# Chunk 1's second product by seven products of quarters, four more blocks transposed by DMA, and new instruction orders, in a decayed-attention and feed-forward kernel

## The chip, the cores and the metric

One Trainium2 chip, one core of it. The metric is device time in microseconds. The kernel before took 211.13 us (median of 3 runs, 210.77 to 211.39).

## The reference

Two stages. The first is causal linear attention with decay for 4 batches, 8 heads, 768 positions, head size 64, in blocks with a running state; the second is a feed-forward layer on the result, seen as 3072 tokens of 512 values.

```python
for b in range(nb):
    intra = np.einsum('bhic,bhjc->bhij', qb, kb) * Dmask[None]
    intra = np.einsum('bhij,bhjd->bhid', intra, vb)
    inter = np.einsum('bhid,bhde->bhie', qb * lam_pow[None], kv_state)
    out[:, :, sl] = intra + inter
    kv_state = lam_block * kv_state + np.einsum('bhsd,bhse->bhde', kb * rev_pow, vb)
x = out.transpose(0, 2, 1, 3).reshape(B * S, H * D)
h = x @ w_in                       # 3072 x 512 by 512 x 2048
s = np.sin(alpha * h)
g = h + s * s / (alpha + 1e-09)
return g @ w_out                   # 3072 x 2048 by 2048 x 512
```

## The kernel before

The tokens are cut into 24 blocks of 128 (6 to a batch) for the attention and into 6 chunks of 512 (4 blocks each) for the feed-forward layer.

**A block of attention.** SP loads q, k and v in float32. `scale_block` (L454 to 496) multiplies q and k by powers of the decay into bfloat16 (`qk2`) and casts v (`v2`). q and k are then transposed into `qkT`: on TensorE, by `piece_Q` (a pair of blocks, L519) and `piece_T` (k of one block, L498) with an eviction each, or, for blocks from `TD` on, by one `dma_start_transpose` on SP (L501). On TensorE follow S (k by q, `part_S`, L612), the masking of S on VectorE (L623, tile `Sm`), the state update Z (L656) with a copy of the state (`Zd`, `Zc`), and the output O (from the state, L694 or L707, and from `Sm`, L716), which is evicted into `xT`, the chunk's input to the feed-forward layer. The first four blocks, one chunk, go through a form of their own (`piece_K`, `piece_P`, `piece_I`) in which tokens are interleaved.

**A unit of the first product.** `unit_A` (L807) multiplies 128 columns of w_in by the 512 tokens of a chunk (4 matmuls, L822); `unit_A2` (L845) does two times 128 columns for 256 tokens (8 matmuls, L856). The result lies in a PSUM bank; ScalarE takes the sine (tile `t16`, L832 and L866), ScalarE or GpSimd squares it (`u16`, L836, L837, L870, L871), and VectorE adds it up into `gT` (L839, L874), after which the bank is free. A chunk has 16 units.

**The second product.** Chunks below `SC` use `unit_B` (L880): for 128 tokens four pieces of 4 matmuls, 512 wide (L887), a copy into `osb` (L901) and a store. Chunks from `SC` on use a product of 2 x 2 quarters with seven products (`unit_P`, L955): 14 pieces of 8 matmuls, 256 wide (L975). It needs sums of quarters of w_out (`weight_sums`, L914, operations at L930, into `ws`, `Ta` and in place in `w2`) and, for each chunk, sums of quarters of `gT` (`token_sums`, L933, operations at L953, into `Xs` and in place in `gT`; 20 for a chunk, 4 of them late). The results are put together by `finish` (L1003) through `kept`: copies (L1012), an addition (L1015) and subtractions into `osb` (L1021).

**The order.** `_Plan` records every operation with its reads and writes. The order on each of the five queues is written out as a table of operation numbers, `ORDER` (L36 to 103); a pair in TensorE's table stands for so many matmuls on an idle tile, which only keep it busy. Where an operation may go to several engines, the table decides. `_settle` merges the tables, and `emit` puts a semaphore wait before whatever reads or overwrites another queue's result. Each queue runs strictly in its order. The durations given to `op` are a planner's; they don't reach the chip.

Loads go by SP (q, k, v and the first quarter of w_in) and GpSimd's queue (the other weights, cast by DMA). Rings hold 6 blocks of k and v, 3 pairs of q, 6 scaled blocks and 6 transposed ones. The input q of the first four blocks and the first quarter of w_in, cast by `cast_w1_first` (L381), are needed before the first unit.

Of the kernel before, what the change touches and what calls it, by code (L numbers as in the profile page):

```python
# [13 lines left out]
class _Op:  # L14


    def __init__(self, eng, emit, dur, reads, writes, dma, after, issue, lat, runs=64):
# [13 lines left out]
        self.knows = None  # L31


class _Plan:
# [17 lines left out]
        ),  # L52
        "ACT": (
# [16 lines left out]
        ),  # L70
        "DVE": (
# [30 lines left out]
        ),  # L102
    }

# [104 lines left out]
def bass_lightning_attn__then__act_snake_kernel(  # L209
# [15 lines left out]
    NB = S // BL  # L225
# [1020 lines left out]
```

## Time and profile before

| | |
|---|---|
| median of the runs | 211.13 us |
| span of the profiled execution | 209.8 us |
| what the median has beyond the span | 1.3 us |
| TensorE busy | 203.5 us |
| VectorE busy | 160.3 us |
| ScalarE busy | 158.7 us |
| GpSimd busy | 126.9 us |

The page of the profile lists busy time by engine (PE is TensorE, PEld its weight loads, DVE VectorE, ACT ScalarE, POOL GpSimd, SP the queue that issues most DMAs). A group's row has line, engine, operation, output<-inputs, sizes and count, then busy us and mean ns of one, then the engine's idle time just before them with what ended it. The chain of waits gives start, length and what. A row of busy time by stretch gives the stretch, its length, then for PE, PEld, DVE, ACT and POOL the busy us (instructions), then the granted clock, the DMA engines' share and GB/s. A row in order of time gives start, length, engine, line, operation and count, with the idle time before it in brackets.

### The profile page before, as it was taken

To read this page: it belongs to the slowest core of one execution; us is meant where nothing else is said; L and a number is where in the kernel's file an instruction comes from. 1 tells how busy PE (TensorE), PEld (TensorE's weight loads), DVE (VectorE), ACT (ScalarE), POOL (GpSimd) and SP (SyncE) were. 2 spreads that over 40 slices of the span, in tenths; PEclk is the share of its full clock that TensorE was granted. 3 is DMA by queue.
4 is the path that set the end of the run, shared out by engine and by line. 5 is a ranking of instruction groups with operands and counts; after the bars stand their busy time and mean duration, and the time that the engine had idled before them with its cause. 6 is when DMAs were issued, how large, how long until landed. Compare 5 with 4: busy or idle time off the path is not lost.

```text
span 209.8 us, 4867 instructions
## 1 busy us (share of the span) xinstructions
PE 203.5 (97%) x1975; PEld 134.3 (64%) x1975; DVE 160.3 (76%) x266; ACT 158.7 (76%) x294; POOL 126.9 (60%) x130
## 2 busy tenths in 40 slices
PE   7979999999999999999998999999999999999995
PEld 6847444457677776555555667766667765666894
DVE  4884557563999866868899799889698699777643
ACT  4949995968998989999997887787963889568210
POOL 7075354994469578679885392944581957378300
DMA  4999999999998999999999920190000004000514
GB/s 141 310 318 232 206 213 237 246 229 256 220 264 205 227 245 230 223 233 196 246 271 228 213 53 0 33 271 2 3 0 3 0 23 179 3 0 0 200 40 163
DMA packets 78998, 33.35 MB, mean 159 GB/s; under 512 B 55408, under 2 KB 76160, under 8 KB 78976
## 3 DMA queue, kind: packets, MB, share of 16 engines
q1 hardware_dynamic: 73744, 27.14, 56.2%
q0 software_dynamic: 3696, 3.67, 10.5%
q10 hardware_dynamic: 1536, 2.24, 3.3%
q8 instruction: 15, 0.25, 0.5%
q14 instruction: 7, 0.06, 0.1%
HBM read 27.28 MB, written 6.29 MB: 160 GB/s over the span
## 4 chain that ended last, share of the span: by engine, by line
PE 83%; DVE 6%; DMA 3%; SPq 3%; ACT 2%; issue 1%
PE bank L822 27%; PE bank L975 22%; PE bank L887 13%; PE bank L856 10%; DMA v<-in_v_dram 3%; PE bank L716 3%; SPq L315 3%; PE bank L612 3%; DVE gT L839 2%; PE bank L694 1%; DVE Sm L623 1%; PE bank L511 1%; PE bank L656 1%; DVE w L930 1%; PE bank L534 1%; PE bank L707 1%
## 5 line engine op out<-in xcount | busy, mean ns | idle before, releaser
L822 PE MATMUL bank<-xT,w 128*128 128x512 bf16 x296 | 70.5, 379 | 0.0
L839 DVE SCALAR_TENSOR_TENSOR gT<-u,rinv,bank 128x512 bf16<-128x512 bf16 x74 | 53.6, 742 | 18.2 <-ACT u L836 12.5
L832 ACT ACTIVATE t<-bank,alpha 128x512 bf16<-128x512 f32 x74 | 50.0, 684 | 21.0 <-PE bank L822 20.5
L822 PEld LDWEIGHTS bank<-xT,w 128*128 128x128 bf16 x296 | 28.3, 98 | 28.4 <-DVE gT L839 0.4
L836 ACT ACTIVATE u<-t 128x512 bf16<-128x512 bf16 x59 | 36.5, 628 | 1.3
L837 POOL TENSOR_TENSOR u<-t 128x512 bf16<-128x512 bf16 x15 | 16.0, 1066 | 34.1 <-ACT t L832 30.5
L953 POOL TENSOR_TENSOR gT<-gT 128x512 bf16<-128x512 bf16 x24 | 27.8, 1172 | 11.2 <-DVE Xs L953 6.0
L623 DVE TENSOR_TENSOR Sm<-bank,mask 128x1024 bf16<-128x1024 f32 x24 | 29.1, 1218 | 4.3 <-PE bank L648 1.8
L887 PE MATMUL bank<-w,gT 128*128 128x512 bf16 x128 | 31.4, 380 | 0.0
L874 DVE SCALAR_TENSOR_TENSOR gT<-u,rinv,bank 128x256 bf16<-128x256 bf16 x44 | 18.8, 476 | 7.8 <-ACT u L870 6.1
L472 POOL TENSOR_TENSOR qk<-q,Lq 128x512 bf16<-128x512 f32 x20 | 21.2, 1075 | 2.8 <-DMA q<-in_q_dram 2.8
L856 PE MATMUL bank<-xT,w 128*128 128x256 bf16 x176 | 22.2, 273 | 0.0
L492 POOL TENSOR_TENSOR qk<-k,Lk 128x512 bf16<-128x512 f32 x20 | 20.9, 1053 | 0.6 <-DMA k<-in_k_dram 0.6
L866 ACT ACTIVATE t<-bank,alpha 128x256 bf16<-128x256 f32 x44 | 18.9, 476 | 2.0 <-PE bank L856 1.5
L887 PEld LDWEIGHTS bank<-w,gT 128*128 128x128 bf16 x128 | 11.7, 98 | 12.2
L856 PEld LDWEIGHTS bank<-xT,w 128*128 128x128 bf16 x176 | 16.4, 98 | 3.5 <-issue 0.3
L953 POOL TENSOR_TENSOR Xs<-gT 128x512 bf16<-128x512 bf16 x13 | 16.1, 1235 | 1.5 <-DVE gT L839 1.4
L975 PE MATMUL bank<-w,gT 128*128 128x256 bf16 (+1 forms) x136 | 16.3, 266 | 0.0
L975 PE MATMUL bank<-w,Xs 128*128 128x256 bf16 (+1 forms) x136 | 16.0, 267 | 0.1
L975 PE MATMUL bank<-ws,gT 128*128 128x256 bf16 x128 | 15.8, 273 | 0.0
L975 PEld LDWEIGHTS bank<-w,gT 128*128 128x128 bf16 x136 | 12.6, 98 | 3.2
L975 PEld LDWEIGHTS bank<-w,Xs 128*128 128x128 bf16 x136 | 12.4, 98 | 2.8 <-DVE osb L1021 0.3
(101 smaller groups left out, 276.0 us busy)
## 6 DMA issues: line engine op xcount, KB each, us to landing
q<-in_q_dram SPq DMA_DIRECT2D x12, 512.0 KB, 6.2
k<-in_k_dram SPq DMA_DIRECT2D x24, 256.0 KB, 5.5
v<-in_v_dram SPq DMA_DIRECT2D x24, 256.0 KB, 5.4
out_dram<-osb SPq DMA_DIRECT2D x14, 256.0 KB, 2.5
w<-in_moe_w_out_dram POOLq DMA_DIRECT2D x4, 512.0 KB, 11.4
w<-in_moe_w_in_dram POOLq DMA_DIRECT2D x3, 512.0 KB, 9.0
ws<-in_moe_w_in_dram SPq DMA_DIRECT2D x2, 512.0 KB, 7.5
out_dram<-osb ACTq DMA_DIRECT2D x8, 128.0 KB, 4.0
```

The source lines that it names most:

```text
L472: lambda e, a=a: e.tensor_tensor(qk2[:, j:j + 2, 4 * a:4 * a + 4, :], q32[:, jq, 4 * a:4 * a + 4, :, :].rearrange("p h t d -> p t h d"), b ...
L492: lambda e: e.tensor_tensor(qk2[:, j, H:2 * H, :], block32(k32, jl), lk, ALU.mult), 1.05,
L623: op("DVE", lambda e: e.tensor_tensor(Sm[js][:, :, :], banks[:, 512 * b0:512 * b0 + 1024].rearrange("p (c i) -> p c i", i=128), bass.AP(ma ...
L822: ins = e.matmul(ps[hb][:, c0:c1], w1[:, kc, 128 * m:128 * (m + 1)], xT[x][:, kc, c0:c1], start=(kc == 0 and c0 == lo), stop=(kc == NKC - ...
L832: op("ACT", lambda e: e.activation(t16[ju][:, w], ps[hb][:, w], ACTF.Sin, scale=alpha[:, m:m + 1]), 0.69 if hi - lo == TCH else 0.475, [ba ...
L836: lambda e: (e.activation(u16[ju][:, w], t16[ju][:, w], ACTF.Square) if e is nc.scalar else e.tensor_tensor(u16[ju][:, w], t16[ju][:, w], ...
L839: op("DVE", lambda e: e.scalar_tensor_tensor(out=gT[g][:, m, w], in0=u16[ju][:, w], scalar=rinv[:, m:m + 1], in1=ps[hb][:, w], op0=ALU.mul ...
L856: ins = e.matmul(ps[hb][:, 256 * i:256 * i + 256], w1[:, kc, 128 * (m + i):128 * (m + i + 1)], xT[x][:, kc, lo:lo + 256], start=(kc == 0 a ...
L866: op("ACT", lambda e, i=i: e.activation(t16[ju][:, 256 * i:256 * i + 256], ps[hb][:, 256 * i:256 * i + 256], ACTF.Sin, scale=alpha[:, m + ...
L887: ins = e.matmul(ps[ob][:, w], gT[g][:, m, 128 * s4:128 * (s4 + 1)], w2[:, m, w], start=(m == 0), stop=(m == NM - 1),)
L953: e.tensor_tensor(dst, in0, in1, alu), 0, rd, wr))
L975: ins = e.matmul(ps[ob][:, lo + d0:lo + d1], lhs, rhs[:, d0:d1], start=first and p == 0, stop=(p == NM // 2 - 1), skip_group_check=True)
```

## The change

Line numbers in this text are those of the kernel before; the changed file is 9 lines longer from L136 to L233 on, and 11 or more behind.

- `SC` from 2 to 1: chunk 1's second product is made by `product` in 14 pieces, with its own 20 token sums and `finish`; both sets of weight sums are made while chunk 1's first product runs, instead of in chunks 2 and 3.
- `TD` from 12 to 8: blocks 8 to 11 are transposed by DMA; a new constant `LB` keeps 12 where the loop over late blocks begins.
- Many operations may now go to other engines: q and k scalings to VectorE or GpSimd (`DP`), v casts to three engines (`ADP`), evictions and copies to ScalarE or VectorE (`AD`).
- All five tables of `ORDER` are new. In them TensorE begins with 31 idle matmuls of 512 columns where it had 42 of 112 and others between; SP loads the first k and v tiles in another sequence and issues the four new transposes between loads; GpSimd makes the decay's exponents after most of its masks; six of the ten weight sums are on GpSimd; VectorE has 295 operations where it had 266, ScalarE 290 where it had 309, GpSimd 135 where it had 132, each with issued DMAs.
- The masks' operations on half the partitions wait for GpSimd's operation before them explicitly (`some`, `strict`) instead of through a common key.

The core of the diff, without the tables:

```diff
-    TD = 12
+    TD = 8
+    LB = 12
...
-    SC = 2
-    QD = ((0, 0), (0, 2), (1, 0), (1, 2))
+    SC = 1
+    AD = (("ACT", 0, 0), ("DVE", 0, 0))
+    DP = (("DVE", 0, 0), ("POOL", 0, 0))
+    ADP = (("ACT", 0, 0), ("DVE", 0, 0), ("POOL", 0, 0))
...
-                    op("DVE",
+                    op(AD,
                        lambda e, lo=lo: (e.copy if e is nc.scalar else e.tensor_copy)(
                            w1[:, :, lo:lo + 256], ws[:, :, lo:lo + 256]), 0.7, [("ws", lo)], [("w1", lo // 256)])
...
-                op("ACT", lambda e: e.copy(osb[jo][:, w], ps[ob][:, w]), 0.59, [bank(ob)], parts)
+                op(AD, lambda e: (e.copy if e is nc.scalar else e.tensor_copy)(osb[jo][:, w], ps[ob][:, w]), 0.59, [bank(ob)], parts)
...
             pieces = pieces_of(8, None, False) + pieces_of(10, 9, False)
+            if SC == 1:
+                weight_sums(True)
+                weight_sums(False)
             for i in range(8):
                 unit_A2(1, 2 * i, 1, (5, 6, 4)[(i + 2) % 3])
+                if SC == 1 and i % 2:
+                    token_sums(1, i // 2)
...
-            block = TD
+            block = LB
             for c in range(2, NCH):
                 n, done = len(bq[c - 1]), 0
                 if c == SC:
-                    P.lead = -100
                     weight_sums(True)
-                    P.lead = 0
-                if c == SC + 1:
+                if c == SC + 1 and SC > 1:
                     weight_sums(False)
...
+        for o in order:
+            if o.eng == "POOL" and o.dma is None:
+                if last is not None and (o.some or last.some):
+                    o.strict = last
+                    o.deps.add(last)
+                last = o
```

More of the change, by code (lines that the diff above doesn't have):

```diff
@@ L31, in __init__ @@
         self.knows = None
+        self.some = False
+        self.strict = None
 class _Plan:
@@ L163, in _ordered @@
     def _ordered(d, o):
-        if d.eng != o.eng or d.dma is not None:
+        if d.eng != o.eng or d.dma is not None or d is o.strict:
             return False
@@ L446, in _ @@
             op("ACT", lambda e: e.copy(alpha[:, :], ps[4][:, 0:NM]), 0.2, [bank(4), "warm"], ["alpha"])
-            def QE(s, a):
-                return "DVE" if (s, a) in QD else "POOL"
             def ported(o):
@@ L478, in scale_block @@
                     for a in range(2) if s % 2 == 0 else ():
-                        eng, dur = ("DVE", 0.68) if s + a < 3 else ("POOL", 1.05)
-                        ported(op(eng, lambda e, a=a: e.tensor_tensor(
+                        ported(op(DP, lambda e, a=a: e.tensor_tensor(
                             qk2[:, j:j + 2, H + 4 * a:H + 4 * a + 4, :],
@@ L483, in scale_block @@
                             bass.AP(Lp, n * H + 4 * a, [[NP * H, 128], [H, 2], [1, 4], [0, D]]), ALU.mult),
-                           dur, [("k32", jl + a), "Lp"], [("k2", j, a), ("k2", j + 1, a)]))
+                           0.68, [("k32", jl + a), "Lp"], [("k2", j, a), ("k2", j + 1, a)]))
                     for a in range(2) if s % 2 == 0 else ():
-                        ported(op("ACT" if s and not a else "POOL", lambda e, a=a: (e.copy if e is nc.scalar else e.tensor_copy)(
+                        ported(op(ADP, lambda e, a=a: (e.copy if e is nc.scalar else e.tensor_copy)(
                             v2[:, j:j + 2, 4 * a:4 * a + 4, :],
@@ L490, in scale_block @@
                     return
-                ported(op("POOL",
+                ported(op(DP,
                    lambda e: e.tensor_tensor(qk2[:, j, H:2 * H, :], block32(k32, jl), lk, ALU.mult), 1.05,
                    [("k32", jl), "Lk"], [("k2", j, 0), ("k2", j, 1)]))
-                ported(op((("ACT", 0.62, 0.0), ("POOL", 1.05, 0.3)) if s > 11 else "ACT",
+                ported(op(ADP,
                    lambda e: (e.copy if e is nc.scalar else e.tensor_copy)(v2[:, j, :, :], block32(v32, jl)), 0.62,
@@ L538, in piece_Q @@
                     if len(tbs) == 2:
-                        op("ACT", lambda e, a=a: e.copy(qkT[:, jt:jt + 2, 2 * a:2 * a + 2, :], tps[a]),
+                        op(AD, lambda e, a=a: (e.copy if e is nc.scalar else e.tensor_copy)(
+                            qkT[:, jt:jt + 2, 2 * a:2 * a + 2, :], tps[a]),
                            0.59, [bank(tbs[a])], [("qT", jt, a), ("qT", jt + 1, a)])
@@ L569, in piece_K @@
                 for t in range(2):
-                    op("ACT" if s else (("DVE", 0.43, 0.0), ("ACT", 0.6, 0.0)),
+                    op(AD,
                        lambda e, t=t: (e.copy if e is nc.scalar else e.tensor_copy)(qkT[:, jt + t, 4:8, :], tps[t]),
@@ L665, in then @@
                         r = slice(64 * h, 64 * h + 64)
-                        op("ACT" if s < NP else (("ACT", 0.36, 0.0), ("DVE", 0.43, 0.0)), lambda e, r=r: (e.copy if e is nc.scalar else e.tensor_copy)(
+                        op(AD, lambda e, r=r: (e.copy if e is nc.scalar else e.tensor_copy)(
                             Zd[s % 2][r, :, r], ps[ZB][r, :].rearrange("p (a b) -> p a b", b=128)[:, :, r] if s < NB else
@@ L1011, in finish @@
                 if i in (1, 3):
-                    op("ACT", lambda e: e.copy(c1 if i == 1 else ny, got), 0.59 if n == 2 else 0.37, [bank(ob)], kc if i == 1 else kn)
+                    op(AD, lambda e: (e.copy if e is nc.scalar else e.tensor_copy)(c1 if i == 1 else ny, got), 0.59, [bank(ob)], kc if i == 1 else kn)
                     return
@@ L1199, in _ @@
                             prep(block + 2)
-                        piece_G(block if block < NBLK else None, block - 1 if block > TD else None,
+                        piece_G(block if block < NBLK else None, block - 1 if block > LB else None,
                                 3 - 3 * (done // 4 % 2) if c <= SC else other())
```

30 lines of the change are left out of this document (16 added, 14 removed), and 111 rows, old and new, of the table ORDER.

## The prediction

> **What bounds the kernel now.** I read the page first, then the chain of work in order of time, then busy time by stretch, then groups by shape.
>
> ```profile
> span 209.8 us, 4867 instructions
> PE 203.5 (97%) x1975; PEld 134.3 (64%) x1975; DVE 160.3 (76%) x266; ACT 158.7 (76%) x294; POOL 126.9 (60%) x130
> PE 83%; DVE 6%; DMA 3%; SPq 3%; ACT 2%; issue 1%
> ```
>
> ```profile
> 14.49 0.62 ACT v L486
> ...
> 19.16 0.87 PE bank L856 x8
> ...
> 39.85 0.45 PE bank L534 x8
> ...
> 52.56 0.22 PE bank L511 x4
> ...
> 81.09 1.73 PE bank L887 x8
> ...
> 136.79 0.87 PE bank L975 x8
> ...
> 193.05 14.14 PE bank L975 x152
> 207.21 0.29 DVE osb L997
> ```
>
> ```profile
> 60.00:70.00 10.00, 10.00 (x118) 7.41 (x117) 9.19 (x18) 9.13 (x20) 8.17 (x9) 1.00 0.92 225
> ...
> 100.00:110.00 10.00, 10.00 (x75) 5.29 (x73) 9.47 (x12) 9.45 (x18) 8.72 (x8) 1.00 1.20 266
> 110.00:120.00 10.00, 9.44 (x84) 6.00 (x82) 8.19 (x13) 8.18 (x14) 4.43 (x5) 1.00 1.09 227
> 120.00:130.00 10.00, 9.89 (x98) 6.43 (x97) 10.00 (x16) 7.53 (x14) 6.95 (x7) 1.00 0.19 35
> ```
>
> Three parts. Up to 19.16 us the first four blocks are loaded and attended, and TensorE waits for others (the chain runs over the last v load and ScalarE). From 19.16 to 207.21 the chain is nearly all TensorE: in the ten-microsecond stretches it idles only in 110 to 130, 0.56 + 0.11 = 0.67 us. The rest, 209.8 - 207.2 = 2.6 us, is the last subtraction and store. The clock is 1.00 throughout. The profiled execution's span of 209.8 stands 1.3 us under the median of 211.13; I take 1.3 as what lies around the span, and sum changes against the median.
>
> So there are two ways to gain: less work on TensorE, or an earlier 19.16. There is one main way to lose: another engine falls behind TensorE in the middle. That is close already: VectorE is busy 9.47 and 10.00 of 10 us in two of the stretches.
>
> **TensorE's saving.** Chunk 1's second product was 16 pieces of four 512-wide matmuls (L887); it becomes 14 pieces of eight 256-wide ones (L975). A pair of the first takes 1.73, so 16 x 0.865 = 13.84; 14 x 0.87 = 12.18. Saving 1.66 us. Blocks 8 to 11 lose two groups of eight transposes (L534, 0.45) and four of four (L511, 0.22 where nothing else delays it; one in three rows of the chain shows 0.3): 2 x 0.45 + 4 x 0.25 = 1.9 us. Together 3.56 us, all of it in the part where the chain is TensorE. It is hidden by nothing, so it counts in full as long as TensorE stays fed.
>
> **The start.** Here the new orders move work onto VectorE.
>
> ```profile
> 1.52 3.55 PE L1134 MATMUL bank<-Xs 128*128 128x112 bf16 x42 [1.52 <-DVE Xs L410]
> ...
> 5.84 2.50 DVE L462 TENSOR_TENSOR qk<-q,Lq 128x512 bf16<-128x512 f32 x4 [1.01 <-ACT Lq L434]
> ...
> 10.70 1.04 POOL L480 TENSOR_TENSOR qk<-k,Lp 128x512 bf16<-128x512 f32 x1 [5.41 <-DMA k<-in_k_dram]
> ...
> 11.27 3.49 DVE L623 TENSOR_TENSOR Sm<-bank,mask 128x1024 bf16<-128x1024 f32 x3 [0.41 <-PE bank L612]
> ...
> 13.61 0.62 POOL L486 CAST v<-v 128x512 bf16<-128x512 f32 x1 [1.31 <-DMA v<-in_v_dram]
> ...
> 15.30 1.23 DVE L623 TENSOR_TENSOR Sm<-bank,mask 128x1024 bf16<-128x1024 f32 x1 [0.54 <-PE bank L612]
> 16.89 0.79 DVE L384 CAST w<-ws 128x1024 bf16<-128x1024 f32 x1 [0.36 <-DMA ws<-in_moe_w_in_dram]
> ...
> 18.99 2.07 PE L856 MATMUL bank<-xT,w 128*128 128x256 bf16 x16
> ```
>
> Before, VectorE masks the four S tiles (L623) from 11.27 to 16.53, and GpSimd scales the last k and casts three v. After, VectorE does all four q and all four k scalings, a v cast and three evictions ahead of the first mask, then the four masks, an x eviction and the first weight cast, and only then the first unit can start. Two things set that mask. (a) VectorE's own sum: eight scalings at 2.50 / 4 = 0.63 are 5.0, the v cast, three evictions and three small casts about 2.1 (estimate from the rows of 0.42 and 0.28 of such copies): 5.84 + 7.1 = 12.9, and some 0.5 later if the exponents come later, since GpSimd now makes them after its masks. (b) The third k tile, sixth in SP's queue before (lam counted), is the ninth now. The ninth of before, a v, released GpSimd at 13.61; so the tile's scaling can start at 13.6, the other k scaling and a mask cast follow, and the first mask starts at 15.1. From there four masks (3.49 / 3 = 1.16 each, 4.65), the eviction (0.7) and the cast (0.7) take 6.05: the first unit starts at 18.95 by (a), 19.4 with the later exponents, and 21.2 by (b), against 18.99. Cost 0 to 2.2 us; I take 1.4, nearer to (b), which rests on a landing that the trace shows. The row of the 42 warming matmuls says that 512-wide ones in their place (31 of them) may hold TensorE to about 10 us, which no later step of (b) notices.
>
> **The middle.** I compare 40 units of the first product, from chunk 1's first to chunk 3's ninth, in the trace 49.55 to 121.27, counting what stands between these marks in each engine's order.
>
> ```profile
> 34.52:120.00 85.48, 84.92 (x832) 52.68 (x831) 66.71 (x109) 74.38 (x145) 61.84 (x56) 1.00 1.09 235
> 49.55:121.27 71.72, 71.16 (x724) 45.77 (x722) 58.75 (x99) 65.14 (x128) 50.24 (x47) 1.00 1.08 229
> ```
>
> ```profile
> L953 DVE TENSOR_TENSOR Xs<-gT 128x512 bf16<-128x512 bf16 x19 | 12.3, 658 | 0.1
> L726 DVE CAST xT<-bank 128x512 bf16<-128x512 f32 x7 | 5.1, 734 | 1.3 <-PE bank L716 1.1 <-PE bank L656 0.3
> L1021 DVE TENSOR_TENSOR osb<-bank,kept 128x512 f32<-128x512 f32 x6 | 4.1, 684 | 0.5 <-PE bank L975 0.5
> L666 DVE CAST Zd<-bank 64x256 bf16<-64x256 f32 x8 | 3.4, 419 | 0.2
> L930 DVE TENSOR_TENSOR w<-w 128x1024 bf16<-128x1024 bf16 x3 | 3.3, 1105 | 0.0
> L462 DVE TENSOR_TENSOR qk<-q,Lq 128x512 bf16<-128x512 f32 x4 | 2.5, 688 | 1.0 <-ACT Lq L434 1.0
> L516 DVE COPY qkT<-bank 128x512 bf16<-128x512 bf16 x5 | 2.1, 424 | 2.3 <-PE bank L511 2.3
> L543 DVE COPY qkT<-bank 128x1024 bf16<-128x1024 bf16 x3 | 2.1, 692 | 0.4 <-PE bank L534 0.4
> ```
>
> ```profile
> L953 DVE TENSOR_TENSOR gT<-gT x24: 409/418/1372, 98.2 to 200.2; 128x512 bf16<-128x512 bf16 x24
> ```
>
> TensorE needs 71.7 there. After, 24 transposes go (1.3) and the two kinds of second product nearly cancel between these marks: about 70.5. VectorE, 58.75 busy, gets 18 token sums more (8 before, 26 after), four scalings of q and k, two v casts, four operations on the products' results (chunk 1's, once ScalarE copies) and three state copies; it loses five evictions of transposes, two of x, two weight sums and a mask. With the rows: 18 x 0.42 + 4 x 0.69 + 1.2 + 4 x 0.68 + 3 x 0.42 = 15.5, less 3 x 0.42 + 2 x 0.69 + 2 x 0.73 + 0.7 + 1.1 + 1.2 = 7.1: 67.2 us if no sum is held up. The sums' row says 418 ns at the median, 658 at the mean of the other form and up to 1372: at about 0.59 each, 70.3. So **VectorE goes from 82% of this stretch to 95 to 100%**. The fullest long-lived share that the stretches show is 9.47 of 10 where TensorE never idled. At that share 67.2 takes 71.0 and 70.3 takes 74.2, that is 0.5 to 3.7 us over TensorE's 70.5. I take 1.5, nearer to the uncollided end, as the token sums are what the new order places anew. The 0.67 us of idle of before lies in this stretch and the one after and is replaced by this.
>
> ScalarE falls: it loses 12 v casts, four output copies and most of the evictions, and 65.1 of 71.7 was its load. GpSimd's total hardly changes.
>
> ```profile
> 107.05 1.16 POOL L953 TENSOR_TENSOR gT<-gT 128x512 bf16<-128x512 bf16 x1
> 107.22 1.27 DVE L953 TENSOR_TENSOR Xs<-gT 128x512 bf16<-128x512 bf16 x1
> ...
> 108.17 2.30 POOL L930 TENSOR_TENSOR w<-w 128x1024 bf16<-128x1024 bf16 x1
> ...
> 109.07 1.95 DVE L930 TENSOR_TENSOR w<-w 128x1024 bf16<-128x1024 bf16 x1
> ```
>
> These four rows show why sums take 0.42 or 1.37: a sum on VectorE that begins during GpSimd's ends some 0.3 us after GpSimd's, and the weight sum at 109.07 ends at 111.02, 0.55 after GpSimd's 110.47. So of two such operations one waits for the other. As a resource: from GpSimd's first scaling to about 120 us, GpSimd is busy 61.84 and VectorE adds some 7 of such operations, 69 of 85.5. After, GpSimd's list to the same place (15 q and 12 k scalings, 15 token and 6 weight sums, 9 casts, two squares, at the durations of before) is 67, and VectorE's (27 token and 4 weight sums, some 9 scalings and casts) 19: **86 of about 85**. [...]
>
> **DMA transposes.**
>
> ```profile
> L501 SPq DMA_TRANSPOSE qkT<-qk x12: 1239/1782/2932, 72.9 to 136.3; - x12
> ...
> DMA to landing us min/median/max: 3.1/4.6/6.7
> ```
>
> Four more of these stand in SP's queue, ahead of the v loads of blocks 9 to 11 and the k loads of 12 and 13, which wait behind them for about 4 x 1.8 = 7 us of SP's time and for GpSimd's scalings. These blocks are attended after block 8, so I cost it at nothing. The cover is that q and k of block 8 are scaled a landing (6.7 at most) before TensorE reaches its S tile; if GpSimd is late, TensorE waits for the difference. The end of the kernel holds the same 14 products of the last chunk: nothing.
>
> **Sum.** -1.66 - 1.90 + 1.4 + 1.5 - 0.67 = -1.3: 211.13 to **209.8**.
>
> **Rivals.** (1) TensorE stays dense and the start isn't late: -3.56, the idle of 0.67 gone or not, start 0 to 0.5: 207.2. For it: TensorE was never idle at a VectorE share of 10.00 in 120 to 130. Against: the start's loads. [...] (3) The DMA transposes are late: GpSimd's scaling of blocks 8 to 11 stands behind six weight sums of 2.1 us; one landing of 4.6 missed by half for two pairs gives 2 us more: 212.0.
>
> **Chances.** Forecast 0.42 (208.6 to 211.2), rival 1 0.20, rival 2 0.30, rival 3 0.08. A measurement tells about 0.3%, 0.63 us, from no change: faster is below 210.5, slower above 211.8. From the forecast 0.30, 0.09, 0.03 (faster, same, slower), rival 1 0.20 faster, rival 2 0.01, 0.03, 0.26, rival 3 0.01, 0.02, 0.05: faster 0.52, same 0.14, slower 0.34. The range is 207.0 to 213.6, from rival 1 to just past rival 2.
>
> **What would show it.** 112 more of L975's matmuls, 64 fewer of L887's, 16 fewer each of L511's and L534's; the first 256-wide unit at 19.4 to 21.2; VectorE above 93% between the marks with TensorE idle there 1 to 2 us; token sums nearer to 0.42 than 0.66. [...]

## The result and the profile after

The changed kernel takes 212.72 us (median of 6 runs, 211.87 to 213.2) against 211.14 for the kernel before (6 runs): ratio 1.0075, 95% interval 1.0057 to 1.0093. It is **slower by 0.75%**, where the prediction had 0.6% faster. Medians are over all executions of a kernel; ratios go by its fast ones, which leaves out those over 1.5% above the kernel's fastest (one each of kernels 7 and 16, three of kernel 11). Line numbers from here on are those of the changed kernel, 8 to 12 higher.

The page of the changed kernel (busy us and share by engine, and the chain that ended last by engine):

```profile
span 211.0 us, 4818 instructions
PE 201.1 (95%) x1927; PEld 135.5 (64%) x1950; DVE 167.5 (79%) x295; ACT 152.7 (72%) x279; POOL 127.9 (61%) x133
PE 69%; DVE 16%; ACT 11%; issue 2%; ACTq 0%
```

TensorE was 83% of that chain and is 69%; VectorE went from 6% to 16% and ScalarE from 2% to 11%. The work did come down, and other engines took the place. (The trace has records of 279 of the 296 matmuls of L831. The chain leaves TensorE where one is missing, so the two grown shares are likely somewhat too high.) Its start, in order of time, on TensorE, VectorE and ScalarE:

```profile
1.66 9.56 PE L1143 MATMUL bank<-Xs 128*128 128x512 bf16 x31 [1.66 <-DVE Xs L421]
...
12.20 0.42 DVE L580 COPY qkT<-bank 128x512 bf16<-128x512 bf16 x1 [0.89 <-PE bank L569]
...
15.27 4.62 DVE L632 TENSOR_TENSOR Sm<-bank,mask 128x1024 bf16<-128x1024 f32 x4
...
18.80 0.62 ACT L494 CAST v<-v 128x512 bf16<-128x512 f32 x1
19.32 1.04 ACT L395 CAST w<-ws 128x1024 bf16<-128x1024 f32 x1
20.39 0.73 ACT L748 CAST xT<-bank 128x512 bf16<-128x512 f32 x1
21.14 0.76 ACT L675 CAST Zd<-bank 64x256 bf16<-64x256 f32 x2
...
21.95 0.40 PE L788 MATMUL bank<-qkT,Zd 128*128 128x128 bf16 x4 [0.64 <-ACT Zd L675]
22.18 1.04 PE L865 MATMUL bank<-xT,w 128*128 128x256 bf16 x8
```

The first unit starts at 22.18 where it was 18.99: 3.2 us late. The 31 warming matmuls end at 11.22, VectorE waits 0.89 for the first transpose behind them, the four masks follow from 15.27, and behind them ScalarE has a cast of v, a cast of the weight, an x and two states in a row. The end, in the chain of waits:

```profile
193.55 14.92 PE bank L984 x160
...
208.50 0.29 DVE osb L1006
```

The last product ends at 208.47, where it was 193.05 + 14.14 = 207.19. So from the first unit to the last product's end it takes 186.3 where it took 188.2. By the counts TensorE has 64 fewer 512-wide matmuls at 0.216, 112 more 256-wide ones at 0.109 and 32 fewer transposes at 0.056: 13.8 - 12.2 + 1.8 = 3.4 us less to do, of which 1.9 arrived. The stretch between the marks of the prediction (chunk 1's first unit and chunk 3's ninth), and VectorE's two fullest pieces (stretch, length, busy us of PE, PEld, DVE, ACT, POOL, clock):

```profile
51.40:122.86 71.46, 69.44 (x744) 49.51 (x753) 65.81 (x122) 63.15 (x124) 53.05 (x51) 1.00 1.09 215
...
100.00:110.00 10.00, 9.24 (x100) 6.10 (x102) 9.87 (x14) 7.34 (x13) 7.88 (x9) 1.00 1.12 216
110.00:120.00 10.00, 9.39 (x82) 6.00 (x82) 9.73 (x19) 8.03 (x14) 5.20 (x6) 1.00 1.28 207
```

VectorE is at 65.81 of 71.46, 92% (82% before). In 100 to 120, where it is at 98%, TensorE idles 1.4 us, of which some 0.5 is three matmuls without a record. What TensorE waited for between 36 and 125 us (line, for what, us, times, longest):

```profile
PE bank L621 <- DVE gT L848: 0.8, 1, 0.8
PE bank L831 <- DVE gT L848: 0.5, 1, 0.5
PE bank L831 <- ACT xT L735: 0.3, 1, 0.3
...
PE bank L831 <- ACT kept L1021: 0.3, 1, 0.3
...
```

The whole list has nine, 2.7 us in all. Six of them stand where one of a unit's four matmuls has no record, while all four weight loads have: five of 0.16 us, in rows left out here, are no waits at all, and of the 0.3 for ScalarE's x, at 109.2, 0.1 is left. So TensorE waits 1.7 us there: 0.8 at 44.8, and behind chunk 1's first unit 0.3 at 100.4 for ScalarE's copy `kept`, 0.1 at 109.2 and 0.5 at 113.9 for a unit sum of VectorE. The kernel before has one there:

```profile
PE bank L694 <- DVE gT L839: 0.6, 1, 0.6
```

The token sums on VectorE and the transposes by DMA, of the changed kernel:

```profile
L962 DVE TENSOR_TENSOR gT<-gT x31: 406/420/633, 81.9 to 199.1; 128x512 bf16<-128x512 bf16 x31
...
L509 SPq DMA_TRANSPOSE qkT<-qk x16: 1243/1524/3545, 60.8 to 141.4; - x16
...
DMA to landing us min/median/max: 3.1/4.1/7.0
```

The longest such sum is 0.63 where it was 1.37, and no wait of TensorE names a transpose by DMA.

### The profile page after: what moved, and what is told of

It is laid out like the page before. It is cut to its first block, busy times and chain, and to the rows that moved or that the text cites. A ratio compares the mean times of both kernels' runs of the same rounds, so it can differ in the third digit from the quotient of the medians.

```text
span 211.0 us, 4818 instructions
## 1 busy us (share of the span) xinstructions
PE 201.1 (95%) x1927; PEld 135.5 (64%) x1950; DVE 167.5 (79%) x295; ACT 152.7 (72%) x279; POOL 127.9 (61%) x133
## 3 DMA queue, kind: packets, MB, share of 16 engines
q0 software_dynamic: 3696, 3.67, 10.8%
## 4 chain that ended last, share of the span: by engine, by line
PE 69%; DVE 16%; ACT 11%; issue 2%; ACTq 0%
PE bank L831 25%; PE bank L984 22%; PE bank L896 5%; PE bank L865 5%; PE bank L1143 5%; DVE gT L883 4%; ACT u L845 3%; DVE Sm L632 3%; ACT t L841 3%; DVE gT L848 3%; PE bank L621 2%; PE bank L725 2%; ACT Zd L675 1%; DVE Xs L962 1%; PE bank L657 1%
## 5 line engine op out<-in xcount | busy, mean ns | idle before, releaser
L831 PE MATMUL bank<-xT,w 128*128 128x512 bf16 x279 | 67.6, 379 | 2.8 <-issue 0.6
L831 PEld LDWEIGHTS bank<-xT,w 128*128 128x128 bf16 x296 | 27.6, 98 | 29.3 <-DVE gT L848 2.2
L962 POOL TENSOR_TENSOR gT<-gT 128x512 bf16<-128x512 bf16 x29 | 33.4, 1159 | 15.9 <-DVE Xs L962 7.6
L846 POOL TENSOR_TENSOR u<-t 128x512 bf16<-128x512 bf16 x12 | 12.4, 1039 | 26.2 <-ACT t L841 25.3
L984 PE MATMUL bank<-w,gT 128*128 128x256 bf16 (+1 forms) x168 | 19.9, 267 | 0.0
L984 PE MATMUL bank<-ws,gT 128*128 128x256 bf16 x160 | 19.9, 273 | 0.0
L984 PEld LDWEIGHTS bank<-w,gT 128*128 128x128 bf16 x168 | 15.9, 98 | 4.3
L500 POOL TENSOR_TENSOR qk<-k,Lk 128x512 bf16<-128x512 f32 x16 | 17.1, 1074 | 1.3 <-DMA k<-in_k_dram 1.3
L984 PEld LDWEIGHTS bank<-w,Xs 128*128 128x128 bf16 x168 | 15.8, 98 | 3.2
L984 PEld LDWEIGHTS bank<-ws,gT 128*128 128x128 bf16 x160 | 15.5, 98 | 3.5
L481 POOL TENSOR_TENSOR qk<-q,Lq 128x512 bf16<-128x512 f32 x15 | 15.5, 1042 | 0.0
L896 PE MATMUL bank<-w,gT 128*128 128x512 bf16 x58 | 14.7, 379 | 0.3
## 6 DMA issues: line engine op xcount, KB each, us to landing
w<-in_moe_w_out_dram POOLq DMA_DIRECT2D x4, 512.0 KB, 10.8
```

What stands on the lines that cost most here:

```text
L500: lambda e: e.tensor_tensor(qk2[:, j, H:2 * H, :], block32(k32, jl), lk, ALU.mult), 1.05,
L831: ins = e.matmul(ps[hb][:, c0:c1], w1[:, kc, 128 * m:128 * (m + 1)], xT[x][:, kc, c0:c1], start=(kc == 0 and c0 == lo), stop=(kc == NKC - ...
L896: ins = e.matmul(ps[ob][:, w], gT[g][:, m, 128 * s4:128 * (s4 + 1)], w2[:, m, w], start=(m == 0), stop=(m == NM - 1),)
L962: e.tensor_tensor(dst, in0, in1, alu), 0, rd, wr))
L984: ins = e.matmul(ps[ob][:, lo + d0:lo + d1], lhs, rhs[:, d0:d1], start=first and p == 0, stop=(p == NM // 2 - 1), skip_group_check=True)
```

## The experiments

All numbers are for one core; a ratio is to the kernel before on the same chip in the same session. The table has, from each profile, the first unit (M0), chunk 1's first unit (M1), chunk 3's ninth (M2) and the last product's end, to some 0.05 us. They are of one execution each, and executions of one kernel differ by up to 3 us: those shown of kernels 4 and 17 were their fastest, that of kernel 1 its slowest.

| kernel | M0 | M1 | M2 | end | median us | ratio, 95% interval |
|---|---|---|---|---|---|---|
| before | 18.99 | 49.55 | 121.21 | 207.18 | 211.1 | |
| changed | 22.19 | 51.40 | 122.86 | 208.46 | 212.72 | 1.0075 (1.0057 to 1.0093) |
| changed, again | 21.54 | 51.11 | 123.31 | 208.91 | 213.36 | 1.0124 (1.0085 to 1.0163) |
| 1 before's start | 18.98 | 53.88 | 125.63 | 211.23 | 213.87 | 1.0132 (1.0092 to 1.0172) |
| 2 short warming row | 22.97 | 52.09 | 122.88 | 208.48 | 213.18 | 1.0104 (1.0065 to 1.0142) |
| 3 = 1, long row | 23.50 | 52.23 | 123.53 | 209.13 | 213.62 | 1.0123 (1.0101 to 1.0145) |
| 4 mask cast early | 21.05 | 49.64 | 120.48 | 206.08 | 211.97 | 1.0046 (1.0024 to 1.0068) |
| 5 = 1, weight load mended | 19.00 | 53.17 | 124.50 | 210.10 | 213.98 | 1.0151 (1.0117 to 1.0185) |
| 6 row of 22 | 22.45 | 51.58 | 123.82 | 209.42 | 214.01 | 1.0137 (1.0115 to 1.0159) |
| 7 = 5, narrow sums | 19.02 | 53.77 | 125.71 | 211.31 | 214.8 | 1.0117 (1.0091 to 1.0143) |
| 8 = 5, changed load order | 23.29 | 52.09 | 123.43 | 209.02 | 213.31 | 1.0113 (1.0098 to 1.0129) |
| 9 = 5, weight sooner | 19.00 | 52.21 | 123.22 | 208.82 | 214.38 | 1.0161 (1.0135 to 1.0188) |
| 10 = 9, long row | 22.91 | 52.74 | 124.07 | 209.67 | 214.1 | 1.0144 (1.0115 to 1.0172) |
| 11 before, long row | 22.86 | 56.19 | 127.54 | 213.50 | see text | |
| 12 before's first 50 us | 18.98 | 51.50 | 124.56 | 210.16 | 215.0 | 1.0189 (1.0163 to 1.0214) |
| 13 = 4, split row | 21.35 | 50.75 | 123.46 | 209.06 | 213.25 | 1.0100 (1.0064 to 1.0137) |
| 14 = 12, sums on VectorE | 18.99 | 50.15 | 123.53 | 209.13 | 213.88 | 1.0134 (1.0102 to 1.0165) |
| 16 = 4, cast off ScalarE | 21.24 | 50.18 | 121.43 | 207.03 | 211.64 | 1.0028 (1.0006 to 1.0050) |
| 17 = 4, narrow sums | 22.23 | 50.74 | 121.79 | 207.40 | 212.6 | 1.0090 (1.0066 to 1.0114) |

From M2 to the end every kernel with the changed order takes 85.6 us, and before takes 86.0: **all differences arise before M2**.

### The start put back: 1, 5 and 9

My first theory was that the 3.2 us of the start simply reach the end. Kernel 1:

```diff
         "PE": (
-            (31, 512), 59, 61, 39, 62, 57, 55, 53, (16, 128), 65, 75, 69, 70, 67, (14, 128), 73, 82, 78, 80, 87,
-            85, 90, 91, 93, 124, 136, 140, 144, 130, ...
+            (42, 112), 39, (30, 128), 57, (11, 128), 55, (1, 128), 53, (1, 128), 59, (8, 128), 61, (1, 512), 62,
+            ... 87, 90, 91, 93, 124, 136, 140, 144, 130, ...
         "ACT", "DVE", "POOL", "SP": likewise the part ahead of the first unit
```

> The changed kernel with the prolog orders of before on all five engines (matmuls to warm up, transposes, masks, first loads, scalings, casts), and everything from the first unit on as changed. Theory S (the changed kernel loses in its start: 3.2 us later at the first unit, which nothing after it gives back; its saving on TensorE is real): first unit at 18.9 to 19.3 again, and all of the 3.2 us reach the end, 212.7 - 3.2 = 209.5 (209.2 to 210.2), faster than before. [...]

Measured 213.87, M0 at 18.98. Theory S fell, and the end is not within 0.6 of the changed kernel's 212.7 either: TensorE waited 3.0 us for the first weight's last quarter. I had put the load behind a GpSimd operation that waits for the first unit, so kernel 5 puts it back:

```diff
 "POOL"
-            52, 105, 106, 127, 104, 197,
+            52, 105, 106, 104, 127, 197,
```

> The first kernel of the set before (before's prolog, the rest as changed) with one GpSimd operation moved: the first square that the change gives to GpSimd stands behind the last early load of the first weight, not ahead of it. In that kernel the load was issued at 21.96 behind the square, landed at 34.1, TensorE waited 2.96 us for it and its granted clock was 0.5 for the 3.4 us that followed. Theory S, corrected (the late start costs all of its 3.2 us, and the rest of that kernel's loss was this load): no wait for the weight, clock 1.00 throughout, first unit at 19.0, and 212.7 - 3.2 for the start - 0.6 for the early mask cast + up to 0.8 for stalls that a later start hid = 209.3 to 209.8. Rival D (loads, with the DMA rings full up to 60 us, hold any earlier start): another load is late in 25 to 50 us, and the time is above 211.

Measured 213.98, and the same wait. The chain of waits of kernel 5 (start, length, what):

```profile
17.89 16.20 DMA w<-in_moe_w_in_dram
...
34.23 1.88 PE bank L831 x4
```

The load is issued 4 us sooner (17.9, not 21.96) and lands at 34.1, as in kernel 1. In the kernel before it landed at 33.4 (issued 18.0, 15.4 us), and TensorE came to it at 35.2, 16.2 us after its first unit; the changed order comes to it after 11.2. In the changed kernel itself (issue, then time to landing):

```profile
L326 POOL DMA_DIRECT2D w<-in_moe_w_in_dram x1: 803/803/803, 25.2 to 25.2; - x1
...
DMA to landing us min/median/max: 8.1/8.1/8.1
```

It lands at 33.3, and is wanted at 22.2 + 11.2 = 33.4: the late start had just hidden it. Kernel 9 takes it ahead of a load of the second weight:

```diff
 "POOL"
-            52, 105, 106, 104, 127, 197,
+            52, 105, 104, 106, 127, 197,
```

> The kernel with before's prolog and the changed rest, once more, now with the first weight's last early load between the two loads of the second weight, as the changed kernel has it, and not behind both. With it behind both it landed at 34.1, and TensorE, which the changed order brings to it 12.6 us after the first unit (16.0 in before), waited 3.1 us; in three of six runs its clock then fell to half for 3.4 us. Theory L (an early start was worth nothing there because the weight was late; with the weight in time all of it counts): landing near 30.5, no wait of over 1 us up to 50 us, clock 1.00, first unit at 19.0; the undisturbed runs of that kernel, 212.8 to 213.5, less 3.1 to 3.6: 209.5 to 210.2, under before's 210.8. Rival D (the DMA rings are full up to 60 us, so that bringing one load forward makes another late): a wait for the second weight of 2 us or more, and over 211.3. Rival M (VectorE and ScalarE from 50 us on take it back): no wait before 50 us, but 1.5 us or more of new ones in 80 to 120, over 211.3.

Measured 214.38, no wait for a weight, and another in its place, in the chain of waits of kernel 9:

```profile
24.78 11.38 DMA q<-in_q_dram
...
36.22 1.56 POOL qk L481
...
37.91 1.01 PE bank L542 x8
```

Now TensorE meets a q that lands at 36.15, GpSimd scales it at 36.22, and TensorE stands 2.7 us. The move did not make this q late: in kernels 1 and 5 it was issued at 24.9 and 24.8 and landed at 36.3 and 36.1 too, and the wait for the weight ahead of it hid that. So rival D held in that another load holds TensorE and the time is above 211.3, but not in that bringing one load forward made this one late. With before's start, the changed order asks the loads for more than they bring. The wait costs twice, which I hadn't counted. The two stretches of kernel 9 around it:

```profile
34.21:37.62 3.41, 1.02 (x5) 0.29 (x3) 1.61 (x3) 2.41 (x4) 1.40 (x1) 1.00 0.92 193
37.62:41.03 3.41, 3.12 (x14) 1.72 (x15) 1.35 (x2) 0.00 (x0) 3.39 (x4) 0.50 0.82 212
```

TensorE is busy 1.02 of 3.41 us, and the granted clock is 0.50 for the next 3.41, which costs half of that, 1.7. Kernel 5's executions show the same sum: 214.5, 215.3 and 215.0 with a mean clock of 0.992, and 213.4, 213.5 and 212.8 with 1.000.

### The warming row: 2, 3, 10, 11, 6, 13

Kernel 2 is the changed kernel with before's first row:

```diff
 "PE"
-            (31, 512), 59, 61, 39,
+            (42, 112), 59, 61, 39,
```

> The changed kernel with only its first warming matmuls replaced by those of before (42 of 112 columns for 31 of 512), so that TensorE is free for transposes from about 5 us and not 11.2. Theory S1 (filler and lists share the loss): VectorE's idle 0.89 us at 12.20 goes, then ScalarE's and VectorE's own lists hold the start: first unit near 21.3, 212.7 - 0.9 = 211.8. Rival F (the filler alone makes the start late): first unit at 19.0 to 19.5, 209.6. Rival L (the lists alone): first unit within 0.3 of 22.2, 212.7.

Measured 213.18 with M0 at 22.97: none of the three. The row ended at 5.7, TensorE was busy 0.24 of the 3.42 us from 5.43, and the clock was 0.50 from 8.85 to 15.67; a group of four transposes (L542) took 0.61 us there and takes 0.39 in the changed kernel. What the long row costs in time it gives in clock. The other way round, kernel 3 is kernel 1 with `(42, 112) -> (31, 512)`:

> The first kernel of this set (before's prolog) with only its 42 warming matmuls of 112 columns replaced by 31 of 512. Theory S1: transposes start at 11.1 and not 7.2, before's masks wait with them: first unit near 21, that is 2 later than with the short filler, 211.6. Rival F: 22.2, 212.7. Rival L: under 0.3 later than with the short filler.

M0 at 23.50, 4.5 later, but 213.62 against 213.87: the late start cost nothing at the end, since the wait for the weight and the half clock went with it. Where the mean clock is 0.999 or more in both, kernel 1 took 212.75, 212.75 and 213.35 and kernel 3 213.4 to 214.3, so some 0.8 of the 4.5 us is left. So I asked the same of kernel 9, whose weight is in time, in kernel 10:

> The kernel above with its 42 warming matmuls of 112 columns replaced by 31 of 512. Theory S (a later start reaches the end where no load hides it): first unit at 23.0 to 23.5, 4.0 to 4.5 later, and 2.5 to 4.0 more at the end (stalls of the middle can hide up to 1.5): 212.5 to 213.7. Rival M: under 1.0 more at the end.

Measured 214.1 against 214.38, with M0 3.9 later. Rival M held. The same edit on the kernel before, kernel 11:

> The kernel before, with the same edit alone: 31 warming matmuls of 512 columns in the place of 42 of 112. Theory S: transposes start at 12 and not at 7.2, the first unit at 23 to 23.5 and not 18.99, and nothing gives it back: 214.3 to 215.3. Rival M: under 212.3.

One execution took 217.81; the other three (221.2 to 222.3) ran at mean clocks of 0.985 to 0.991. In the first M0 is 3.9 later and the end 6.3 later: there nothing gives a late start back, and TensorE waits 2.8 for VectorE besides. So in the changed order a start between 19.0 and 23.5 is **worth next to nothing** at the median (0.8 at most, in kernels 1 and 3), in the order of before it is worth all of it and more.

Kernel 6 shortens the row only a little:

```diff
 "PE"
-            (31, 512), 59, 61, 39,
+            (22, 512), 59, 61, 39,
```

> The changed kernel with 22 instead of 31 warming matmuls of 512 columns. In its profile they took 0.427 us each up to 7.0 us and 0.216 from there, and held TensorE to 11.2; in the run with the early mask cast the clock rose at 4.9 and they ended at 9.9. Theory W (the end of the warming row depends on when the clock rises, so it costs 0 to 1.2 us at the first unit, another amount in every execution; past that the lists and the third k bound the start): the row ends by 9.1 at the latest, first unit at 21.0 to 21.1, clock 1.00, 211.8 to 212.4, with less spread than the changed kernel's 1.3 us. Rival V (the clock falls back, as with the short row): clock under 1.00 in 10 to 26 us and no gain. Rival L (lists alone): 212.7.

Measured 214.01: the row ends at 7.9, TensorE waits 1.3 for a q, is busy 1.46 of the 3.41 us from 7.79, and the clock is 0.50 from 11.2 to 14.6. Rival V. Kernel 13 splits the row, on kernel 4:

```diff
 "PE"
-            (31, 512), 59, 61, 39, 62, 57, 55, 53,
+            (21, 512), 59, (3, 512), 61, (1, 512), 39, 62, (2, 512), 57, 55, 53,
```

> The kernel with the third mask cast early, and its warming row of 31 matmuls split: 21 ahead of the first transposes, and 3, 1 and 2 between them, so that TensorE is kept busy and transposes can start from 9 us. Theory W (the warming row costs 0 to 1.2 us, by when the clock rises): clock 1.00, first unit at 21.0 to 21.2 in the profile; that kernel's median of 212.0 less 0.5: 211.2 to 211.8, and less spread than its 2.9 us. Rival V (TensorE is then too little busy and the clock falls back): clock below 1.00 in 8 to 18 us, first unit past 22, over 212.3.

Neither held. In the profile the clock stayed at 1.00 and M0 is 21.35, no earlier than kernel 4's, and the time is 213.25. From M1 to M2 it is 72.7, where kernel 4's fastest execution takes 70.8; TensorE waits 1.1 there for a sum of VectorE and 0.8 for ScalarE's `kept`. How long the row of 31 holds TensorE differs by execution. Kernel 4's row, against the 9.56 above:

```profile
1.66 8.38 PE L1143 MATMUL bank<-Xs 128*128 128x512 bf16 x31 [1.66 <-DVE Xs L421]
```

In the changed kernel's profile the matmuls of this row took 0.427 us each up to 7.0 and 0.216 from there; in kernel 4's the step came at 4.9. The first unit follows 11.0 us behind the row's end in both, and 10.9 to 11.1 behind it in kernels 16 and 17 and in the repetition, where the row ends at 10.3, 11.3 and 10.4.

### The load order: 8

```diff
 "SP", on kernel 5
-            0, 2, 3, 4, 5, 6, 7, 8, 9, 10, 11, 96, 97,
+            0, 3, 4, 5, 2, 9, 7, 8, 6, 11, 10, 97, 96,
```

> The first kernel of this set with only SP's order of the first eleven loads as in the changed kernel (q and k of the first two blocks ahead, the third k as the ninth). Theory B (the third k's landing sets the first masks, as the prediction's step (b) had it): the first unit at 20.5 to 21.1, and 1.5 to 2.1 us more than the first kernel of this set. Rival L (the lists of the engines alone make the changed kernel's start late): first unit at 19.0 to 19.4, within 0.4 of the first kernel.

M0 at 23.29, but TensorE's 3.1 us wait was for a q scaling, and the clock was 0.50 from 10.8 to 14.2. The run does not single out the third k. The median is 213.31 against 213.98: once more a start 4.3 later costs nothing.

### The mask cast: 4

```diff
 "DVE"
-            66, 68, 74, 79, 86, 98, ... 145, 182, 28, 194,
+            66, 68, 74, 79, 28, 86, 98, ... 145, 182, 194,
```

> The changed kernel with one cast moved: the third mask, which VectorE cast at 41.6 in 1.76 us while GpSimd ran a weight sum, is cast right behind the first four mask multiplications, in idle time of VectorE. Theory P (units 14 to 16 lose 0.8 to 1.0 us because that cast meets GpSimd's weight sum and holds the sums behind it): the cast takes 0.2 to 0.3, units 14 to 16 gain 0.5 to 0.8, and 0.5 to 0.8 reach the end: 212.0. Rival Q (the wait moves to the next operation, or is given back by 60 us): less than 0.2 at the end.

VectorE and GpSimd in the changed kernel, then VectorE in kernel 4:

```profile
41.63 1.76 DVE L436 CAST mask<-maskf 128x128 bf16<-128x128 f32 x1
43.31 1.39 DVE L848 SCALAR_TENSOR_TENSOR gT<-u,rinv,bank 128x512 bf16<-128x512 bf16 x2
```

```profile
40.17 2.13 POOL L939 TENSOR_TENSOR ws<-w 128x1024 bf16<-128x1024 bf16 x1
42.25 1.05 POOL L500 TENSOR_TENSOR qk<-k,Lk 128x512 bf16<-128x512 f32 x1
```

```profile
18.68 0.21 DVE L436 CAST mask<-maskf 128x128 bf16<-128x128 f32 x1
```

A cast of 0.21 takes 1.76 while GpSimd works, and ends 0.09 after GpSimd's second operation; the unit sums behind it are late, and so is TensorE. Moved, M0 to M1 falls from 29.2 to 28.6. TensorE's wait of 0.8 for that unit sum stands in the profiles of the changed kernel, its repetition and kernels 2 and 6, and in none of 4, 13, 16 and 17, which have the cast early (13 waits 0.7 for a load there). So theory P's mechanism is shown. The median is 211.97, and the ratio to before falls from 1.0075, or 1.0124 in the repetition, to 1.0046: 0.6 us or more, of which the first is just within the two intervals. The prediction's four rows had this for sums; here it is a cast, 1.76 for 0.21.

### Before's first 50 us: 12 and 14

Kernel 12 takes the tables of before for operations 0 to 248, which both kernels have, and merges the changed ones behind by their start times:

```diff
 "PE" (and the other four likewise: operations 0 to 248 as in before, the rest as changed)
-            ... 93, 124, 136, 140, 144, 130, 147, ... 245, 235, 226, 241, 252, 265, 249, 250, 273, 258,
+            ... 93, 124, 130, 140, 136, 151, 155, ... 237, 241, 221, 245, 226, 252, 265, 249, 250, 273, 258,
```

> The changed kernel with the orders of before on all engines for everything that both have up to the first unit of chunk 1 (the first 249 operations, some 50 us), and the changed orders from there on, merged by their start times. Theory O (the changed order reaches the units that need the first weight's last quarter 11.2 us after the first unit, and a transpose of q at 15.4, where before does at 16.2 and 20.5, and the loads cannot be that early): no wait for a load, clock 1.00, first unit at 19.0, chunk 1's first unit near 50.8 (49.1 in before, and two units more ahead of it), end of the matmuls at 205.3 to 206.3, and 209.2 to 210.3. Rival M (work that the change adds behind 50 us takes it back): 211 or more, with stalls of 2 us or more between 55 and 125 us.

Measured 215.0: theory O fell. From the first unit to 39.9 us TensorE follows before's to 0.05 us; then it waits 1.7 for a q scaling on GpSimd, behind a weight sum of 2.12 which the change brings forward into this stage. Kernel 14 gives four such sums to VectorE:

```diff
 "POOL", on kernel 12
-            199, 330, 195, 329, 196, 197, 331, 211, 212, 213, 219, 281, 332, 276,
+            199, 195, 196, 197, 211, 212, 213, 219, 281, 276,
 "DVE"
-            174, 186, 190, 208, ... 222, 333, 227, 251, 257,
+            174, 330, 186, 329, 190, 208, ... 222, 331, 333, 227, 251, 332, 257,
```

> The kernel with before's first 50 us ahead of the changed rest, with four of chunk 1's weight sums (2.12 us each on GpSimd, three of them between 35.5 and 46.7 and one at 53.6) moved to VectorE, into gaps of 1 to 2.5 us that its trace shows there. Theory G (the weight sums that the change brings forward into 35 to 55 us fill GpSimd, the q scalings behind them are late, and that is what an early start runs into): no wait of TensorE over 0.7 us between 36 and 51, chunk 1's first 256-wide unit near 50.8 less the 3 us lost, that is 48 to 49.5, and 215.0 - 3 = 211 to 212.3. Rival R (more than that): less than 1.5 us gained.

That wait is gone, M1 is 50.15, the earliest but kernel 4's, and the median is 213.88: 1.1 gained, rival R. TensorE's longest waits in kernel 14 between 36 and 125 us are two for unit sums of VectorE (1.4 together) and one for an x of VectorE (1.3). M1 to M2 takes 73.4, the longest of all. A merge by start times is not a tuned order, so this suggests that the start and the rest must be arranged together; it does not show that they can't be.

### Between the marks: 7, 17 and 16

Kernels 7 and 17 narrow chunk 1's in-place token sums, on kernels 5 and 4. Their outputs lack most of these twelve sums; six are on VectorE, which take 0.21 us for 0.42, and six on GpSimd, 0.32 for 1.16:

```diff
+                    if c == 1 and wr[0][0] == "gT":
+                        dst, in0, in1 = dst[:, :, 0:32], in0[:, :, 0:32], in1[:, :, 0:32]
```

> The first kernel of this set with the in-place token sums of chunk 1 (not the ones that go to the sum buffers) narrowed from 512 to 64 elements, so it leaves out most of that part of chunk 1's sums. [...]

> The changed kernel with the third mask cast early, and chunk 1's in-place token sums narrowed from 512 to 64 elements; it leaves out most of that part of chunk 1's sums. [...]

Kernel 7 took 212.95, 213.79, 215.82 and 217.75, where the first two ran at a mean clock of 1.000; kernel 5 took 212.8 to 213.5 at that clock. Kernel 17 took 212.6 where kernel 4 takes 211.97. From M1 to M2 they need 71.9 and 71.1 where their bases have 71.3 and 70.8: no gain. I had looked for 0.7 to 1.2 us less in kernel 7 and 0.8 to 1.5 less in kernel 17, and neither came: chunk 1's in-place sums, on VectorE or on GpSimd, are not what holds TensorE there; the other token sums were not tried. The other candidate is ScalarE; kernel 16 takes one cast of v off it:

```diff
 "ACT", on kernel 4
-            518, 519, 440, 527,
+            518, 519, 527,
 "POOL"
-            475, 382, 478,
+            475, 382, 440, 478,
```

> The changed kernel with the third mask cast early, and the cast of v that ScalarE does at 90.3 given to GpSimd, into a gap of 2.2 us there. Theory A (ScalarE's list holds TensorE in 85 to 101): 0.4 to 0.6 less than that kernel's 212.0, 211.4 to 211.6. [...]

The chain of waits of the changed kernel from 87 us, and of kernel 16 in the same place:

```profile
87.31 0.70 ACT t L841
...
88.03 1.15 ACT u L845 x2
89.17 0.58 ACT t L841
89.78 0.63 ACT u L845
90.41 0.39 ACT v L503
90.82 0.69 ACT t L841
```

```profile
87.66 0.58 DVE gT L848
88.24 0.08 issue
88.32 0.74 DVE gT L848
89.06 0.60 DVE osb L1030
```

ScalarE is out of the chain here, and VectorE stands in it instead, from 85.83 to 93.32 with pauses of 0.09. The only wait of TensorE over 0.15 us between 36 and 125 us in kernel 4 is for ScalarE:

```profile
PE bank L831 <- ACT kept L1021: 0.3, 1, 0.3
```

Kernel 16 has none for this copy, and 0.26 for a sum of VectorE at 112.3 (its other rows stand where a matmul has no record). The median is 211.64, 0.33 less than kernel 4's, less than the two intervals tell apart. So it looks as if both engines were at the edge and relieving one showed the other, but with one profile of each kernel that is not shown. It has the lowest ratio of the changed order, and is still 0.28% slower than before (0.06% to 0.50%).

### The changed kernel again: 15

> The changed kernel again, with nothing edited: 212.7 within 0.5 at the median, single executions over 1.3 to 2.5 us, and in its profile a warming row that ends between 9.9 and 11.3, with the first unit 11.0 to 11.2 us behind that end.

Measured 213.36, a little over the 0.5 I allowed, 212.6 to 215.0; the row ends at 10.41 and the first unit starts 11.1 behind it. TensorE's longest wait here is 1.0 for ScalarE's `kept` at 100.9, where the first profile had 0.3. The changed order is not only slower but wider: 1.3 us in its first six runs, 2.4 here and 2.9 in twelve runs of kernel 4, where seventeen runs of before beside the last span 1.2.

## Why the prediction was wrong

I had 1.33 us less and measured 1.58 more, 2.9 us off. By the profiles 1.8 of it is the start, 0.7 the waits behind it, 0.2 the saving (3.4 and not 3.56), and 0.3 what lies behind the last product and around the span.

**The work on TensorE: right within 0.2 us.** 3.56 us were to go, and 3.4 do by the counts. From M2 to the end little changes (85.6 for 86.0), and from M1 to M2 the changed order has been seen at 70.8 (kernels 2 and 4), where I had put its need at 70.5.

**The start: wrong, by 1.8 us, over its bound.** I gave 0 to 2.2 and took 1.4; it is 3.2. The step of this term that failed is the sentence that the 31 matmuls may hold TensorE to about 10 us, "which no later step of (b) notices". They end at 11.22, and VectorE's eviction at 12.20 waits for the transpose behind them. VectorE in kernel 4, where they end at 10.0, and then in the changed kernel:

```profile
12.61 1.29 DVE L488 TENSOR_TENSOR qk<-k,Lp 128x512 bf16<-128x512 f32 x2 [0.19 <-DMA k<-in_k_dram]
13.83 0.22 DVE L436 CAST mask<-maskf 128x128 bf16<-128x128 f32 x1
14.15 4.62 DVE L632 TENSOR_TENSOR Sm<-bank,mask 128x1024 bf16<-128x1024 f32 x4
```

```profile
13.33 1.28 DVE L488 TENSOR_TENSOR qk<-k,Lp 128x512 bf16<-128x512 f32 x2
14.54 0.63 DVE L436 CAST mask<-maskf 128x128 bf16<-128x128 f32 x1
```

In kernel 4 the third k is waited for, as in (b), but at 12.61 and not 13.6, and for 0.19 only: without it VectorE's own list, path (a), would have brought the masks to some 14.0, where I had 12.9 to 13.4. In the changed kernel no k is waited for. The row brings the scalings 0.7 later, and the mask cast, now beside a cast of v on GpSimd (14.45 to 15.09), takes 0.63 for 0.22. The masks start at 15.27, close to my 15.1, by luck and for another reason. From the masks' start to the first unit it is 6.9 in both, and not 6.05: in the changed kernel VectorE waits 0.56 for an output of TensorE ahead of the eviction of x, and TensorE 0.64 for the last state in ScalarE's list (v, weight, x, states). The sum: masks 2.88 later than the 11.27 of before by lists and k, 1.12 more by the row, and 0.8 less from the masks on. That my upper bound of 21.2 is near kernel 4's 21.05 is luck too: 0.95 too late and 0.85 too short cancel.

**The middle: 0.7 too small, wrong in cause, and in part in the wrong place.** I took 1.5 less the 0.67 of before, 0.8 more of waits. Of the 3.4 us saved, 1.9 arrived: 1.5 more than before. I had VectorE above 93% and its sums as the cost. It is at 92% (65.8 us busy, where I had 67.2 to 70.3), the sums take 0.42, and narrowing chunk 1's in-place ones gains nothing. Kernel 3 between its marks:

```profile
52.23:123.53 71.30, 70.27 (x753) 49.59 (x753) 68.26 (x123) 63.21 (x124) 52.80 (x51) 1.00 1.02 208
```

There VectorE is at 96% and TensorE is held for 1.0 us only (0.3 in kernel 2, also at 96%), so the share by itself is no bound. Of the 1.7 us of waits listed in the changed kernel 0.8 lie ahead of the first mark, where a mask cast met a weight sum, a collision I hadn't looked for. Behind the mark 0.4 are for ScalarE, which I had as relieved since its total falls, and 0.5 for VectorE. The wait for ScalarE's `kept` near 100 us is 0.3 here, 1.0 in the repetition and in kernel 6, and absent in kernel 2. The operations of GpSimd and VectorE of which one waits for the other, which I had at 86 of 85 us, did not fill the stretch: from 34.5 to 120 us GpSimd is busy 62.6 (67 forecast), and it and VectorE's sums, scalings and casts of v and masks together cover 76 of 85.5, counted instruction by instruction in the trace. (For rival 1 I wrote that TensorE was never idle in 120 to 130; its row has 9.89 of 10.)

**The transposes by DMA: right.** No wait names them.

**The sum itself.** I added the start to the middle as if each reached the end by itself. Starts from 19.0 to 23.5 give M2 at 122.9 to 125.7 in every kernel with the changed order but 4, 16 and 17 (120.5 to 121.8), and the earlier ones are not the earlier at M2. With an early start the loads (kernels 1, 5, 9), GpSimd's weight sums (12) and VectorE (14) stop TensorE; with a late one they have time. So the late start of the changed kernel is not 3.2 us that could be had back, and the runs show not one bound, but several that come up in turn. The upper end of the range, 213.6, asks for 3.8 us more than the forecast; no run shows that much in the middle: from M1 to M2 the kernels took 70.8 to 73.4, at most 2.9 over TensorE's 70.5, where I had put 1.5 over it.

**What stays open.** What sets each execution's waits between M1 and M2 (70.8 to 72.7 with nearly the same orders), and which engine's list would have to give way there. No version here beats the kernel before.

## What to carry to other kernels

When an order is changed, ask of each stage what it will find late if it comes sooner: a load, a sum, a clock. A term for the start and one for the middle may not be added until it is shown that nothing between them absorbs or repeats either. A total that falls (ScalarE's, here by 6 us) does not rule out waits for that engine in a stretch where its list is full.

## What the runs showed of the hardware

In the changed kernel's profile 512-wide matmuls took 0.427 us each up to 7.0 us into the span and 0.216 from there; in kernel 4's the step came at 4.9. (The granted clock has no record ahead of the step, and the rows of the profile print 1.00 there.) Later the clock fell back to 0.50 for 3.41 us, or 6.83 in kernels 2 and 7, and in the 3.41 us ahead of such a fall TensorE was busy 0.24, 0.49, 1.01, 1.02 or 1.46 us (kernels 2, 5, 8, 9, 6). In kernel 12 it was busy 1.62 of the 3.41 us from 39.00, and the clock stayed at 1.00.

In kernels 1 and 5 a load's landing hardly depended on its issue while the DMA engines were full (a share of 1.23 from 20 to 30 us in kernel 1, of 1.20 from 30.65 to 34.06 in kernel 5): the first weight's last quarter, issued at 21.96 and 17.9 behind the same other loads, landed at 34.1 both times. The load one place ahead of it on its queue in kernel 5, issued at 16.7, landed at 30.4. In kernel 9, where it takes that place, no wait of TensorE names it.
